# A hand-written engine order for the second layer of a fused attention and two-layer network kernel

## The chip, the cores and the metric

The kernel runs on one core of a Trainium2 chip. The metric is the device time of one execution in microseconds. Before the change it is 1295.35 us, the median of three runs (1294.71 to 1295.54).

## The reference

Chunked attention (chunks of 64, softmax inside each chunk) feeds two dense layers; the second one ends in a softmax-weighted normalization. Tokens: 4608. All data are float32. The part that the change touches is the second layer:

```python
x = _attn_ref(q, k, v)                      # 4608 x 512
h = x @ w_in;  y = (h * np.cos(h)) @ w_out  # first layer, 512 -> 2048 -> 512
h = y @ w_in2                               # second layer, 512 -> 1024
e = np.exp(h - np.max(h, axis=-1, keepdims=True))
solu = h * e / (np.sum(e, axis=-1, keepdims=True) + 1e-09)
mu = np.mean(solu, axis=-1, keepdims=True)
var = np.mean((solu - mu) ** 2, axis=-1, keepdims=True)
out = (((solu - mu) / np.sqrt(var + 1e-06)) * g_ln) @ w_out2
```

## The kernel before, in words

TensorE multiplies in a reduced float format, so every operand is split into a high part (ACT copies it into the format) and a low part (DVE subtracts): `split`, L115. A product is then three matmuls: high by high, high by low, low by high.

The first layer works on blocks of 512 tokens. `evac_y` (L690) writes its result y to DRAM as seven operands per pair of token tiles, the operands of a Strassen-like scheme with seven products in place of eight.

The second layer works on 18 **pairs** of tiles of 128 tokens. A pair has four **segments** (`pair`, L890). Each computes one or two of the seven products (`prod`, L874: 6 matmuls each; segment 2 has one product, the others two) into a PSUM tile of two banks and adds them into the two halves of two tiles h2 on DVE. Segment 0 also copies its first product into h2 on ACT (L918). Some of the sums yield a running maximum as well, called tp. PSUM tiles come from `ps_y` (two buffers) and `ps_a` (one) in turn, so a segment of pair 3 or later takes the buffer of the segment three before it. `load_y` (L726) and `split_y` (L731) fetch and split a pair's y.

For each tile e of a pair, `stats` (L935) negates the maximum (nm, DVE), takes the exp (ACT, L941), multiplies (DVE, L945), squares (ACT, L950) and takes the variance to the power -0.5 on POOL (L955, L956). `norm` (L959) applies it (ACT), `blocks32` (L970) transposes blocks of 32 on DVE into bt. After every second pair `shuffle` (L985) moves bt by 16 DMAs on SP's queue into four tiles lt of 128 tokens. `split_ln` (L996) splits such a tile into lh (ACT) and ll (DVE). `mm_o` (L1001) multiplies it by the output weights in two halves of 12 matmuls, and `store` (L1012) copies the result (ACT) and sends it out by four DMAs.

What sets the order: at L1106 one loop runs over the segments of all pairs from pair 3, segment 1. `segment(i, seg)` (L1020) does segment seg of pair i, the stats of one tile of pair i-1 at even segments and its norm and blocks at odd ones, and loads or splits the next y. Beside it run the two halves of output tile t = 2i - LAG2 + seg // 2, with LAG2 = 7. The first three pairs and segment 0 of pair 3 are done inside the loop of the first layer. In all of this the instructions' places on each engine are left to a scheduler, which takes a ready instruction by priority. `InOrder` (L99) is a wrapper of an engine whose instructions stay in the order in which they are written while `ordered[0]` is true; before the change it is true only for the first stage of the kernel.

Of the kernel before, what the change touches and what calls it, by code (L numbers as in the profile page):

```python
# [29 lines left out]
def kernel(  # L30
# [695 lines left out]
    def load_y(i):  # L726
        t = sp_.tile([P, 7 * 256], F32, tag="st", name="yr")
        nc.sync.dma_start(out=t, in_=y_dram[i // 2][i % 2])
        yr[i] = t
# [19 lines left out]
    if True:  # L749
# [124 lines left out]
        def prod(i, ps, operand, key):  # L874
            for kk in range(2):
                a, b = (y[i][operand][:, kk * P:(kk + 1) * P] for y in (yh, yl))
                whi, wlo = w2in[key, kk]
                nc.tensor.matmul(out=ps, lhsT=a, rhs=whi, start=kk == 0, stop=False)  # L878
                nc.tensor.matmul(out=ps, lhsT=a, rhs=wlo, start=False, stop=False)  # L879
                nc.tensor.matmul(out=ps, lhsT=b, rhs=whi, start=False, stop=kk == 1)  # L880
# [9 lines left out]
        def pair(i, seg):  # L890
# [4 lines left out]
            if seg == 0:  # L895
                h2tile(i, 0)
                h2tile(i, 1)
# [3 lines left out]
            def add(o, ps, other, top=None):  # L901
                if top is None:
                    nc.vector.tensor_tensor(out=o, in0=ps, in1=other, op=ALU.add)
                else:
                    m, before = top
                    nc.vector.tensor_tensor_reduce(  # L906
# [8 lines left out]
            if seg == 0:  # L915
                prod(i, x, 0, "w11")
                prod(i, y, 1, "w12")
                nc.scalar.activation(out=b0, in_=x, func=AF.Copy)  # L918
                add(a0, y, b0, peak(0, 0))
            elif seg == 1:  # L920
                prod(i, x, 4, "s2")
                prod(i, y, 5, "s3")
                add(b0, x, b0)
                add(a1, y, b0)
            elif seg == 2:
                prod(i, x, 3, "s1")
                add(b1, x, a1, peak(1, 0))
                add(b0, x, b0)
            else:
                prod(i, x, 6, "w22")  # L930
                prod(i, y, 2, "s4")
# [3 lines left out]
        def stats(i, e):  # L935
            h2 = hA.pop((i, e))
            nm = ap_.tile([P, 1], F32, tag="nm", name="nm", bufs=4)
            ss = ap_.tile([P, 1], F32, tag="ss", name="ss", bufs=4)
            nc.vector.tensor_scalar(out=nm, in0=tops.pop((i, e, 1)), scalar1=-1.0, scalar2=None, op0=ALU.mult)
            ex = ap_.tile([P, 1024], F32, tag="t", name="e", bufs=2)  # L940
            nc.scalar.activation(out=ex, in_=h2, func=AF.Exp, bias=nm, accum_out=ss)  # L941
            nc.vector.tensor_scalar(out=ss, in0=ss, scalar1=1e-9, scalar2=None, op0=ALU.add)
            nc.vector.reciprocal(out=ss, in_=ss)
            mu = ap_.tile([P, 1], F32, tag="mu", name="mu", bufs=4)
            nc.vector.scalar_tensor_tensor(  # L945
                out=h2, in0=h2, scalar=ss, in1=ex, op0=ALU.mult, op1=ALU.mult, accum_out=mu
            )
            nc.vector.tensor_scalar(out=mu, in0=mu, scalar1=-1.0 / F2, scalar2=None, op0=ALU.mult)
            va = ap_.tile([P, 1], F32, tag="va", name="va", bufs=4)
            nc.scalar.activation(out=ex, in_=h2, func=AF.Square, bias=mu, accum_out=va)  # L950
            nc.vector.tensor_scalar(
                out=va, in0=va, scalar1=1.0 / F2, scalar2=1e-6, op0=ALU.mult, op1=ALU.add
            )
            rs = ap_.tile([P, 1], F32, tag="rs", name="rs", bufs=4)
            nc.gpsimd.tensor_tensor(out=rs, in0=va, in1=nhalf, op=ALU.pow)  # L955
            nc.gpsimd.tensor_tensor(out=mu, in0=mu, in1=rs, op=ALU.mult)  # L956
            solu[i, e], nmu[i, e], rstd[i, e] = h2, mu, rs

        def norm(i, e):  # L959
            so = solu[i, e]  # L960
            nc.scalar.activation(
                out=so, in_=so, func=AF.Identity, scale=rstd.pop((i, e)), bias=nmu.pop((i, e))
            )

# [3 lines left out]
        def blocks32(i, e):  # L970
# [8 lines left out]
            if j:  # L979
                nc.vector.transpose(out=blks[j][4][:, :, n], in_=src)  # L980
            else:
                for c in range(4):
                    nc.vector.transpose(out=blks[j][c][:, :, n], in_=src[:, 8 * c:8 * (c + 1)])
# [12 lines left out]
        def split_ln(j, a):  # L996
            hi, lo = wtile(F32R, "lh"), wtile(F32R, "ll")
            split(lnp.pop((j, a)), hi[:], lo[:])
            lnh[j, a], lnl[j, a] = (x.rearrange("p (f c) -> p f c", c=P) for x in (hi, lo))

        def mm_o(j, a, half):  # L1001
# [3 lines left out]
            for f in range(half * NF2 // 2, (half + 1) * NF2 // 2):  # L1005
                hi, lo = lnh[j, a][:, f], lnl[j, a][:, f]
                whi, wlo = w2out[f]
                nc.tensor.matmul(out=o, lhsT=hi, rhs=whi, start=(f == 0), stop=False)  # L1008
                nc.tensor.matmul(out=o, lhsT=hi, rhs=wlo, start=False, stop=False)  # L1009
                nc.tensor.matmul(out=o, lhsT=lo, rhs=whi, start=False, stop=(f == NF2 - 1))  # L1010

        def store(j, a):  # L1012
            s = gp.tile([P, DM], F32, tag="gh", name="os")
            nc.scalar.activation(out=s, in_=ops.pop((j, a)), func=AF.Copy)
# [28 lines left out]
        for n in range(NSTEP + LAG + 1):  # L1043
# [53 lines left out]
            if rest >= 6:  # L1097
# [6 lines left out]
        first_seg = 4 * EARLY + 1  # L1104
        split_ln(0, 0)
        for x in range(first_seg, 2 * (NI + LAG2) + 4):  # L1106
            i, seg = divmod(x, 4)
            segment(i, seg)
            t, half = 2 * i - LAG2 + seg // 2, seg % 2
            if half == 0:  # L1110
                if 0 <= t + 1 < NI:
                    split_ln(*divmod(t + 1, SUB))
                if 0 <= t - 1 < NI:
                    store(*divmod(t - 1, SUB))
            if 0 <= t < NI:
                mm_o(*divmod(t, SUB), half)
# [27 lines left out]
```

## Time and profile before

| | |
|---|---|
| median of three runs | 1295.35 us (1294.71 to 1295.54) |
| the profiled execution, its own time | 1296.76 us |
| its span, first to last instruction | 1295.0 us |
| mean granted clock of TensorE | 0.987 |
| PE busy | 1251.0 us, 97% |
| DVE busy | 953.8 us, 74% |
| ACT busy | 834.3 us, 64% |
| second-layer matmuls of `mm_o` | 864, of them in the profile 288 at each of L1008, L1009, L1010 |

The second layer overlaps the first layer's end up to about 929 us and then has the chip to itself. A row of the timeline has the start in us from the span's start, the duration, the engine, the line, the operation with output and inputs, and in brackets the engine's idle time before it and what released it. A line L105 is that of the wrapper `InOrder`, so tiles tell such instructions apart. A matmul's 0.39 us is its own duration; matmuls overlap, and their starts are closer together.

### The profile page before, as it was taken

The page shows a single profiled execution, that of the slowest core. Times are in us where ns is not written, and L with a number is a line of the kernel's source. Part 1 is how long each engine was busy: PE and PEld are TensorE (multiplying, and loading weights), DVE is VectorE, ACT ScalarE, POOL GpSimd, SP SyncE. Part 2 cuts the span into 40 slices and gives each one's busy share as a digit, 9 for nine tenths or more (in the row PEclk, how much of TensorE's full clock was granted, in tenths as well). Part 3 has the DMA queues.
Part 4 walks back from the last instruction along what each step waited for, and adds up shares of the span by engine and source line. Part 5 has one row for each costly group of instructions (what it writes and reads, how often), then busy time and mean ns, then how long its engine had stood idle before and what let it go on. Part 6 is the DMA issues. An engine that isn't in the chain of part 4 may idle for free.

```text
span 1295.0 us, 20476 instructions
## 1 busy us (share of the span) xinstructions
PE 1251.0 (97%) x7556; PEld 1007.4 (78%) x7556; DVE 953.8 (74%) x1532; ACT 834.3 (64%) x1231; POOL 124.4 (10%) x271
## 2 busy tenths in 40 slices
PE   5899999999999999999999999999979999999998
PEld 4666778888887777878788888888868888888886
DVE  5987989776778879858868866657786677766851
ACT  5877886656666757647757656557666565666552
POOL 0000000022022022022022012000010000000000
PEclk7999999999999999999999999999989999999999
DMA  9952354342352553562562610641564453435224
GB/s 241 218 112 97 98 141 97 82 102 37 71 155 79 136 148 85 143 146 61 118 129 73 142 31 17 211 159 67 165 179 104 132 147 100 128 90 148 62 70 104
DMA packets 247075, 149.75 MB, mean 116 GB/s; under 512 B 179904, under 2 KB 220352, under 8 KB 245440
## 3 DMA queue, kind: packets, MB, share of 16 engines
q1 hardware_dynamic: 240736, 142.02, 42.8%
q0 software_dynamic: 6144, 6.30, 2.0%
q8 instruction: 59, 0.97, 0.3%
q14 instruction: 40, 0.33, 0.1%
q10 hardware_dynamic: 96, 0.13, 0.0%
HBM read 83.63 MB, written 39.58 MB: 95 GB/s over the span
## 4 chain that ended last, share of the span: by engine, by line
PE 67%; DVE 17%; ACT 8%; issue 3%; DMA 3%; SPq 2%; POOL 0%; DVEq 0%; ACTq 0%; POOLq 0%
PE h L615 6%; PE h L616 6%; PE h L617 6%; PE y L678 6%; PE y L677 6%; PE y L679 6%; PE o L1010 5%; PE o L1008 5%; PE o L1009 5%; PE h L878 4%; PE h L880 4%; PE h L879 4%; DVE z L105 3%; DVE r L630 2%; SPq L105 2%
## 5 line engine op out<-in xcount | busy, mean ns | idle before, releaser
L615 PE MATMUL h<-xh,whi 128*128 128x512 f32 x576 | 228.6, 397 | 2.4 <-ACT xh L105 1.4
L617 PE MATMUL h<-xh,wlo 128*128 128x512 f32 x576 | 225.7, 392 | 0.0
L616 PE MATMUL h<-xl,whi 128*128 128x512 f32 x576 | 225.2, 391 | 0.0
L678 PE MATMUL y<-gl,whi 128*128 128x512 f32 x544 | 214.2, 394 | 4.3 <-DVE gl L105 4.1
L677 PE MATMUL y<-gh,whi 128*128 128x512 f32 x544 | 214.1, 397 | 1.7 <-ACT gh L105 1.1
L679 PE MATMUL y<-gh,wlo 128*128 128x512 f32 x544 | 212.5, 391 | 0.0
L639 ACT ACTIVATE r<-r 128x512 f32<-128x512 f32 x144 | 91.0, 632 | 117.9 <-DVE r L633 117.6
L534 POOL DMA_DIRECT2D ptb<-ptr x192 | 95.4, 504 | 698.4 <-DVE ptr L527 344.1
L105 ACT ACTIVATE gh<-hs 128x512 fp32r<-128x512 f32 x136 | 85.6, 629 | 102.7 <-DVE hs L647 97.2
L647 DVE SCALAR_TENSOR_TENSOR hs<-r,hs 128x512 f32<-128x512 f32 x136 | 93.1, 684 | 65.1 <-ACT r L640 64.8
L630 DVE SCALAR_TENSOR_TENSOR r<-kt,hs 128x512 f32<-128x512 int32 x144 | 99.1, 688 | 47.7 <-ACT kt L629 47.4
L615 PEld LDWEIGHTS h<-xh,whi 128*128 128x128 f32 x576 | 108.6, 189 | 27.6 <-issue 2.3
L616 PEld LDWEIGHTS h<-xl,whi 128*128 128x128 f32 x576 | 108.7, 189 | 23.9 <-issue 1.4
L105 DVE TENSOR_TENSOR gl<-hs,gh 128x512 fp32r<-128x512 f32 x136 | 93.1, 685 | 46.2 <-ACT gh L105 46.0
L617 PEld LDWEIGHTS h<-xh,wlo 128*128 128x128 f32 x576 | 108.6, 188 | 23.1 <-DVE wlo L105 0.2
L678 PEld LDWEIGHTS y<-gl,whi 128*128 128x128 f32 x544 | 102.4, 188 | 29.9 <-DVE gl L105 9.5
L677 PEld LDWEIGHTS y<-gh,whi 128*128 128x128 f32 x544 | 102.2, 188 | 26.1 <-ACT gh L105 2.8
L679 PEld LDWEIGHTS y<-gh,wlo 128*128 128x128 f32 x544 | 102.4, 188 | 21.2 <-DVE wlo L105 0.3
L1008 PE MATMUL o<-whi,lh 128*128 128x512 f32 x288 | 113.4, 394 | 1.6 <-ACT lh L105 1.6
L1010 PE MATMUL o<-whi,ll 128*128 128x512 f32 x288 | 113.3, 393 | 0.8 <-DVE ll L105 0.8
L1009 PE MATMUL o<-wlo,lh 128*128 128x512 f32 x288 | 113.0, 392 | 0.0
L878 PE MATMUL h<-whi,yh 128*128 128x512 f32 x252 | 99.6, 395 | 10.5 <-DVE tp L906 10.5
(113 smaller groups left out, 2162.2 us busy)
## 6 DMA issues: line engine op xcount, KB each, us to landing
lt<-bt SPq DMA_DIRECT2D x144, 128.0 KB
yr<-yd SPq DMA_DIRECT2D x18, 896.0 KB
yd<-ts SPq DMA_DIRECT2D x18, 512.0 KB
out<-os SPq DMA_DIRECT2D x142, 64.0 KB
vi<-in_v SPq DMA_DIRECT2D x64, 128.0 KB
qi<-in_q SPq DMA_DIRECT2D x224, 32.0 KB
ki<-in_k SPq DMA_DIRECT2D x224, 32.0 KB
ptb<-ptr POOLq DMA_DIRECT2D x192, 32.0 KB, 1.7
```

The lines of the kernel that those rows point to most:

```text
L105: ins = getattr(self.engine, name)(*args, **kwargs)
L615: nc.tensor.matmul(out=t, lhsT=wa, rhs=xh[j][:, kk, :], start=(kk == 0), stop=False)
L616: nc.tensor.matmul(out=t, lhsT=wa, rhs=xl[j][:, kk, :], start=False, stop=False)
L617: nc.tensor.matmul(out=t, lhsT=wb, rhs=xh[j][:, kk, :], start=False, stop=(kk == KD - 1))
L630: nc.vector.scalar_tensor_tensor(out=r, in0=kt, scalar=-TWO_PI_HI, in1=h, op0=ALU.mult, op1=ALU.add)
L677: nc.tensor.matmul(out=o, lhsT=wa, rhs=a, start=head, stop=False)
L678: nc.tensor.matmul(out=o, lhsT=wa, rhs=b, start=False, stop=False)
L679: nc.tensor.matmul(out=o, lhsT=wb, rhs=a, start=False, stop=last)
L878: nc.tensor.matmul(out=ps, lhsT=a, rhs=whi, start=kk == 0, stop=False)
L1008: nc.tensor.matmul(out=o, lhsT=hi, rhs=whi, start=(f == 0), stop=False)
L1009: nc.tensor.matmul(out=o, lhsT=hi, rhs=wlo, start=False, stop=False)
L1010: nc.tensor.matmul(out=o, lhsT=lo, rhs=whi, start=False, stop=(f == NF2 - 1))
```

## The change

The scheduler no longer sets the order of the second layer from pair 3 on. `ordered[0]` is set, all matmuls, ACT and DVE instructions of the second layer go through the wrappers, and a new loop writes the order out, one step per pair i. Segment 0 of pair 3 moves from the first layer's loop into it. `pair` is cut into `pair_mm`, `pair_copy` and `pair_sum`, and `stats` into `st_exp`, `st_mul`, `st_square` and `st_var`, with the same instructions in each. `split_ln` can do its high (half 0) or low part (half 1) alone. The load of pair 4's y goes to POOL's queue, ahead of the loop; later loads stand at the end of a step.

```diff
-            if rest >= 6:
+            if 6 <= rest < 6 + 4 * EARLY:
                 segment((rest - 6) // 4, (rest - 6) % 4)
...
         LAG2 = 7
-        first_seg = 4 * EARLY + 1
-        split_ln(0, 0)
-        for x in range(first_seg, 2 * (NI + LAG2) + 4):
-            i, seg = divmod(x, 4)
-            segment(i, seg)
-            t, half = 2 * i - LAG2 + seg // 2, seg % 2
-            if half == 0:
-                if 0 <= t + 1 < NI:
-                    split_ln(*divmod(t + 1, SUB))
-                if 0 <= t - 1 < NI:
-                    store(*divmod(t - 1, SUB))
-            if 0 <= t < NI:
-                mm_o(*divmod(t, SUB), half)
+        load_y(EARLY + 1, nc.gpsimd)
+        ordered[0] = True
+        for i in range(EARLY, NI // 2 + (LAG2 + 1) // 2 + 1):
+            p, t = i - 1, 2 * i - LAG2
+            new, old = i < NPAIR, EARLY - 1 <= p < NPAIR
...
+            if i == EARLY:
+                split_o(t + 1, 0)
+            if new:
+                pair_mm(i, 0)
+            half_o(t, 0)
+            if old:
+                st_exp(p, 0)
+                st_exp(p, 1)
+            store_o(t - 1)
+            split_o(t + 1, 1)
+            if old:
+                st_mul(p, 0)
+                st_square(p, 0)
+            if new:
+                pair_copy(i)
+            if old:
+                st_mul(p, 1)
+            if new:
+                pair_sum(i, 0)
+            if old:
+                st_square(p, 1)
+                st_var(p, 0)
+                st_var(p, 1)
+            if new:
+                pair_mm(i, 1)
+            half_o(t, 1)
+            if old:
+                norm(p, 0)
+                norm(p, 1)
+                blocks32(p, 0)
+            if new:
+                pair_sum(i, 1)
+            if i == EARLY:
+                split_y(i + 1)
+            if old:
+                blocks32(p, 1)
+                if p % 2:
+                    shuffle(p // 2)
+            split_o(t + 2)
+            if new:
+                pair_mm(i, 2)
+            half_o(t + 1, 0)
+            if EARLY < i and i + 1 < NPAIR:
+                split_y(i + 1)
+            if new:
+                pair_sum(i, 2)
+            store_o(t)
+            split_o(t + 3, 0)
+            if new:
+                pair_mm(i, 3)
+            half_o(t + 1, 1)
+            if new:
+                pair_sum(i, 3)
+            if i + 2 < NPAIR:
+                load_y(i + 2)
```

`split_o`, `half_o` and `store_o` call `split_ln`, `mm_o` and `store` where their tile t exists.

PE where the first output tile (o) meets the last segment of pair 3 (h2_9255; in the changed kernel h2_9266). Before:

```order
L879 MATMUL h2_9212<-wlo_8369,yh_9143 128x512
L880 MATMUL h2_9212<-whi_8368,yl_9144 128x512
L878 MATMUL h2_9255<-whi_8472,yh_9143 128x512
L1008 MATMUL o_9242<-whi_8852,lh_9188 128x512
L1009 MATMUL o_9242<-wlo_8853,lh_9188 128x512
L879 MATMUL h2_9255<-wlo_8473,yh_9143 128x512
```

And now:

```order
L105 MATMUL o_9247<-whi_8856,lh_9156 128x512
L105 MATMUL o_9247<-wlo_8857,lh_9156 128x512
L105 MATMUL o_9247<-whi_8856,ll_9157 128x512
L105 MATMUL h2_9266<-whi_8472,yh_9143 128x512
L105 MATMUL h2_9266<-wlo_8473,yh_9143 128x512
```

The last segment stood right behind segment 2; it now stands behind twelve matmuls of output tile 0, and no output matmul stands inside it.

DVE at the same place: the end of pair 2's stats and pair 3's first sum, whose product is h2_9149 (in the changed kernel h2_9159). Before:

```order
L945 SCALAR_TENSOR_TENSOR h2_8929,mu_9229<-h2_8929,ss_9223,e_9225 128x1024
L951 TENSOR_SCALAR va_9177<-va_9177 128x1
L948 TENSOR_SCALAR mu_9229<-mu_9229 128x1
L951 TENSOR_SCALAR va_9232<-va_9232 128x1
L980 STREAM_TRANSPOSE bt_9208<-h2_8928 128x32x32
L980 STREAM_TRANSPOSE bt_9208<-h2_8929 128x32x32
L906 ISA h2_9150,tp_9165<-h2_9149,h2_9151 128x512
```

And now:

```order
L105 SCALAR_TENSOR_TENSOR h2_8941,mu_9193<-h2_8941,ss_9178,e_9180 128x1024
L105 TENSOR_SCALAR mu_9193<-mu_9193 128x1
L105 ISA h2_9190,tp_9198<-h2_9159,h2_9191 128x512
L105 ISA tp_9198 128x1
L105 TENSOR_SCALAR va_9188<-va_9188 128x1
L105 TENSOR_SCALAR va_9200<-va_9200 128x1
L105 STREAM_TRANSPOSE bt_9225<-h2_8940 128x32x32
```

The sum moves ahead of both transposes and of the variances.

DVE at the last sums of pair 17, the last pair (their product is h2_11836; in the changed kernel h2_11841). Before:

```order
L906 ISA h2_11701,tp_11849<-h2_11836,h2_11701,tp_11716 128x512
L906 ISA tp_11849 128x1
L980 STREAM_TRANSPOSE bt_11773<-h2_11507 128x32x32
L906 ISA h2_11702,tp_11851<-h2_11836,h2_11702,tp_11794 128x512
L906 ISA tp_11851 128x1
L980 STREAM_TRANSPOSE bt_11773<-h2_11508 128x32x32
L939 TENSOR_SCALAR nm_11867<-tp_11849 128x1
```

And now:

```order
L105 ISA h2_11753,tp_11866<-h2_11841,h2_11753,tp_11761 128x512
L105 ISA tp_11866 128x1
L105 ISA h2_11754,tp_11868<-h2_11841,h2_11754,tp_11829 128x512
L105 ISA tp_11868 128x1
L105 TENSOR_SCALAR nm_11883<-tp_11866 128x1
```

The two transposes of pair 16 no longer stand between pair 17's last sums and nm.

## Rows read from the trace of the kernel before

**Rows 1.** Busy time by stage: us; PE, PEld, DVE, ACT, POOL; clock, DMA share, GB/s

```profile
1000.00:1050.00 50.00, 49.45 (x218) 40.61 (x218) 36.70 (x80) 29.60 (x42) 3.71 (x10) 1.00 0.50 141
```

**Rows 2.** Timeline of PE, the end: start us, us, line, operation

```profile
1245.38 0.39 PE L1008 MATMUL o<-whi,lh 128*128 128x512 f32 x1
...
1264.19 0.39 PE L1010 MATMUL o<-whi,ll 128*128 128x512 f32 x1
...
1290.30 0.39 PE L1010 MATMUL o<-whi,ll 128*128 128x512 f32 x1
```

**Rows 3.** Timeline of PE, the handover

```profile
938.26 0.39 PE L880 MATMUL h<-whi,yl 128*128 128x512 f32 x1
...
945.25 0.79 PE L878 MATMUL h<-whi,yh 128*128 128x512 f32 x1 [6.60 <-DVE tp L906]
...
950.22 0.39 PE L1010 MATMUL o<-whi,ll 128*128 128x512 f32 x1
```

**Rows 4.** Busy time in three short stretches of the handover, columns as in rows 1

```profile
936.00:938.00 2.00, 2.00 (x10) 1.69 (x9) 1.85 (x7) 1.10 (x2) 0.00 (x0) 1.00 1.03 284
...
946.00:948.00 2.00, 2.00 (x7) 1.49 (x5) 1.84 (x4) 0.00 (x0) 0.00 (x0) 0.50 0.80 305
...
952.00:954.00 2.00, 2.00 (x11) 1.64 (x10) 0.80 (x2) 0.00 (x0) 0.00 (x0) 1.00 0.00 0
```

**Rows 5.** The chain that ended last, one piece: first and last of seven

```profile
988.32 0.60 ACT h L918
...
1238.38 0.60 ACT h L918
```

**Rows 6.** Timeline of PE in one pair

```profile
989.70 0.50 PE L878 MATMUL h<-whi,yh 128*128 128x512 f32 x1 [0.55 <-DVE tp L906]
```

**Rows 7.** Timeline of PE after the last shuffle

```profile
1267.47 0.72 PE L1010 MATMUL o<-whi,ll 128*128 128x512 f32 x1 [0.53 <-DVE ll L105]
...
1270.97 0.40 PE L1009 MATMUL o<-wlo,lh 128*128 128x512 f32 x1
```

**Rows 8.** Timeline of DVE and ACT, the last pair and the last shuffle

```profile
1246.30 1.24 DVE L980 STREAM_TRANSPOSE bt<-h 128x1024 f32<-128x1024 f32 x1
...
1256.80 2.48 DVE L980 STREAM_TRANSPOSE bt<-h 128x1024 f32<-128x1024 f32 x2 [0.98 <-ACT h L961]
...
1265.11 1.05 ACT L105 ACTIVATE lh<-lt 128x1024 fp32r<-128x1024 f32 x1
...
1266.19 1.23 DVE L105 TENSOR_TENSOR ll<-lt,lh 128x1024 fp32r<-128x1024 f32 x1 [6.92 <-ACT lh L105]
```

**Rows 9.** Timeline of ACT, the handover

```profile
934.73 1.16 ACT L941 ACTIVATE e<-h,nm 128x1024 f32<-128x1024 f32 x1 [4.60 <-DVE nm L939]
...
938.05 1.15 ACT L950 ACTIVATE e<-h,mu 128x1024 f32<-128x1024 f32 x1 [0.94 <-DVE ss L943]
...
940.87 2.45 ACT L961 ACTIVATE h<-h,mu,rs 128x1024 f32<-128x1024 f32 x2
...
943.23 0.58 ACT L918 ACTIVATE h<-h 128x512 f32<-128x512 f32 x1
```

**Rows 10.** Timeline of DVE, the handover

```profile
938.14 1.28 DVE L945 SCALAR_TENSOR_TENSOR h<-h,ss,e 128x1024 f32<-128x1024 f32 x1
...
942.12 2.48 DVE L980 STREAM_TRANSPOSE bt<-h 128x1024 f32<-128x1024 f32 x2 [0.98 <-ACT h L961]
...
944.52 0.65 DVE L906 CUSTOM_DVE_ANT_0 h<-h,h 128x512 f32<-128x512 f32 x1
```

**Rows 11.** Timeline of SP's queue, the handover

```profile
935.70 8.76 SPq L990 DMA_DIRECT2D lt<-bt  x11
...
944.50 1.07 SPq L728 DMA_DIRECT2D yr<-yd  x2
```

**Rows 12.** Tile ptb: issues by POOL (duration ns min/median/max), and landing

```profile
L534 POOL DMA_DIRECT2D ptb<-ptr x192: 498/498/838, 268.5 to 794.6; - x192
...
DMA to landing us min/median/max: 1.6/1.7/8.5
```

More of the change, by code (lines that the diff above doesn't have):

```diff
@@ L724, with load_y @@
     yr, yh, yl = {}, {}, {}
[L726 removed]
+    def load_y(i, queue=None):
         t = sp_.tile([P, 7 * 256], F32, tag="st", name="yr")
[L728 removed]
+        (queue or nc.sync).dma_start(out=t, in_=y_dram[i // 2][i % 2])
         yr[i] = t
@@ L877, in prod @@
                 whi, wlo = w2in[key, kk]
-                nc.tensor.matmul(out=ps, lhsT=a, rhs=whi, start=kk == 0, stop=False)
-                nc.tensor.matmul(out=ps, lhsT=a, rhs=wlo, start=False, stop=False)
-                nc.tensor.matmul(out=ps, lhsT=b, rhs=whi, start=False, stop=kk == 1)
+                pe.matmul(out=ps, lhsT=a, rhs=whi, start=kk == 0, stop=False)
+                pe.matmul(out=ps, lhsT=a, rhs=wlo, start=False, stop=False)
+                pe.matmul(out=ps, lhsT=b, rhs=whi, start=False, stop=kk == 1)
         def h2tile(i, e):
@@ L888, in h2tile, with pair_mm @@
             return hA[i, e]
-        def pair(i, seg):
+        h2ps = {}
+        def pair_mm(i, seg):
             c = 4 * i + seg
@@ L895, in pair, with pair_copy, pair_sum @@
             if seg == 0:
-                h2tile(i, 0)
-                h2tile(i, 1)
+                prod(i, x, 0, "w11")
+                prod(i, y, 1, "w12")
+            elif seg == 1:
+                prod(i, x, 4, "s2")
+                prod(i, y, 5, "s3")
+            elif seg == 2:
+                prod(i, x, 3, "s1")
+            else:
+                prod(i, x, 6, "w22")
+                prod(i, y, 2, "s4")
+            h2ps[i, seg] = x, y
+        def pair_copy(i):
+            h2tile(i, 0)
+            h2tile(i, 1)
+            act.activation(out=hA[i, 1][:, HALVES[0]], in_=h2ps[i, 0][0], func=AF.Copy)
+        def pair_sum(i, seg):
+            x, y = h2ps.pop((i, seg))
             a, b = hA[i, 0], hA[i, 1]
@@ new lines, in pair, with col, st_exp @@
+        def pair(i, seg):
+            pair_mm(i, seg)
+            if seg == 0:
+                pair_copy(i)
+            pair_sum(i, seg)
+        small_ = {}
+        def col(i, e, name):
+            t = small_[i, e, name] = ap_.tile([P, 1], F32, tag=name, name=name, bufs=4)
+            return t
+        def st_exp(i, e):
+            nm, ss = col(i, e, "nm"), col(i, e, "ss")
+            dve.tensor_scalar(out=nm, in0=tops.pop((i, e, 1)), scalar1=-1.0, scalar2=None, op0=ALU.mult)
+            ex = small_[i, e, "ex"] = ap_.tile([P, 1024], F32, tag="t", name="e", bufs=2)
+            act.activation(out=ex, in_=hA[i, e], func=AF.Exp, bias=nm, accum_out=ss)
@@ L994, in shuffle, with split_ln @@
                 lnp[j, a] = l
[L996 to L999, printed above, removed]
+        def split_ln(j, a, half=None):
+            if half != 1:
+                lnh[j, a], lnl[j, a] = wtile(F32R, "lh"), wtile(F32R, "ll")
+            split(lnp[j, a], lnh[j, a][:], lnl[j, a][:], half=half)
         def mm_o(j, a, half):
```

77 lines of the change are left out of this document (40 added, 37 removed).

## The prediction

> **What bounds the kernel now.** I read the busy time by stage first. In the second layer TensorE (PE) is busy 49.45 us of 50 at full granted clock, VectorE (DVE) 36.70 and ScalarE (ACT) 29.60 [rows 1]. So PE sets the end there, and only what interrupts it can be won. A busy share does not tell PE's pace, so the timeline comes next. Between its last second-layer product and the stall near the end PE issues 84 matmuls from 1245.38 to 1264.19 us, 83 steps of 0.2266 us [rows 2]. I take 0.2266 us for a matmul throughout.
>
> The changed stretch begins at the handover. After the matmul at 938.26 PE has 1464 matmuls to go: 12 products of pair 3, 42 for each of 14 pairs, 24 for each of 36 output tiles. At the pace above they take 331.7 us. From 938.49 (one step after that matmul) to 1290.53 (one step after the last, [rows 2]) 352.0 us pass. So 20.3 us are lost, and I can place nearly all of them.
>
> - Handover: the next matmul starts at 945.25 where 938.49 was due, 6.76 us late, and waits for DVE's tp, the first sum of pair 3 [rows 3]. After that pause the granted clock is 0.50, which is 1.2 GHz [rows 4]: 10 matmuls take 4.97 us to 950.22 instead of 2.27 [rows 3]. That is 2.70 more, 9.5 us in all. Some 0.35 us follow where the y operands of pair 4 come late.
> - Every second pair: ACT's copy of the first product recurs from 988.32 to 1238.38 in six periods of 41.68 us [rows 5]; 180 matmuls need 40.79. The 0.89 us between them is PE waiting for the tp of the same segment, because the last segment's product is put in front of the output matmuls that could cover the wait [rows 6]. There are seven such places: 6.2 us.
> - The last shuffle: the matmul due at 1264.42 and the next run late, the third only at 1267.47, 2.60 us lost; eight steps to 1270.97 then take 3.50 us instead of 1.81 [rows 7]. Together 4.3 us.
>
> The sum is 9.5 + 0.35 + 6.2 + 4.3 = 20.3 us.
>
> **The change part by part.** No matmul, sum or transfer is added or removed; all of it is order and queue. So I follow each wait in the new order.
>
> *Steady pairs.* I set time 0 at a pair's first matmul. PE now has a fixed row: product 0, 12 output matmuls, product 1, 12, product 2 (6 matmuls), 12, product 3, 12; products start at 0, 5.44, 10.88 and 14.95 us and the next pair at 20.39. A product needs the PSUM tile of the product three earlier, so product 3 needs the first sum of its own pair. That sum comes behind two exps, a store, a square and the copy on ACT. Worked from the durations in [rows 8 to 10]: the previous pair's last sums end at -1.1, the exps at 1.6, the copy at 4.1, the first sum at 4.9. Product 3 starts at 14.95, so the old wait has 10 us of cover. The y split of the next pair ends near 14.5, needed at 20.39. DVE fits 27% idle time into its row [rows 1], so it does not fall behind. I take the seven 0.89 us at nothing: gain 6.2 us. If that cover failed, the 6.2 us would remain (a rival below).
>
> *Handover.* DVE now does the first split of an output operand between nm and the exps. ACT stood idle 4.60 us there, and the first exp ended at 935.9 [rows 9], so a split of 1.23 us [rows 8] starting at 934.76 ends when DVE would have gone on anyway. Costed at nothing; if the exps came sooner it would cost 1.2 us. Then the order that matters: in the old one DVE did two transposes (2.48 us) from 942.12 before the sum of pair 3 at 944.52 [rows 10]; ACT did both squares and both norms before the copy at 943.23 [rows 9]. In the new one the copy follows the first square (938.05 + 1.15, so 939.3 to 939.9) and the sum follows the second product with e, which ends at 939.4: about 940.0 to 940.75. Meanwhile PE no longer waits with product 3 next in line: 12 output matmuls of tile 0 come first, 938.49 to 941.2. Product 3 starts at 941.2, the second 12 at 943.9, pair 4 at 946.65. The 6.76 and the 2.70 us go.
>
> *What is late next there* is pair 4's y. Its load of 0.92 MB stood on SP's queue, which issued it at 944.50, behind 11 shuffle transfers that took from 935.70 [rows 11]. It moves to POOL's queue, past SP's 16 shuffle and 2 last yd transfers. On POOL it stands ahead of the two small operations of pair 2's variance, which now wait behind its issue. Its buffer comes free when the first yd writes have landed and DVE's last ts sum is done, about 935.5. The trace has no such load from POOL; the nearest rows are the 192 small ones, 504 ns to issue, 1.7 us to land, 8.5 at most [rows 12]. I scale the issue to four of those, 2 us, to 937.6; the variance operations are due at 940.9, so 3 us are spare. For landing there are two bounds: alone at the 284 GB/s that the stretch moves [rows 4], 3.2 us, at 940.8; behind everything on SP's queue, at about 951, since DMA is quiet from 952 on [rows 4]. I take an equal share with SP's queue, 6.5 us, landing at 944.1, nearest to the small loads, which did not wait for SP's queue to empty. ACT reaches yh at 944.2 anyway (behind both norms); yh's first part takes 1.05 and yl's 1.23 [rows 8], so yl is ready at 946.8. PE needs it at its third matmul, 947.1. Then pair 4's first 12 output matmuls need the split of tile 1, which DVE ends at about 950.2 behind yl and a transpose; PE is there at 949.8: 0.4 us. Handover gain: 9.5 + 0.35 - 0.4 = 9.4 us.
>
> A load from POOL could also be held back by DVE, busy without a pause until 940.9; that is part of the late-load rival below. The Trainium skill (SBUF — State Buffer, section "SBUF: two separate sides") has a rule of this kind: GpSimd writes the descriptors of its own loads, and can't while DVE runs an operation in a mode that takes the port which the two share. The rows lean against it: DVE needs 1.28 us for 1024 columns there [rows 10], no less than elsewhere, so no such mode shows.
>
> *Tail.* The old order put both transposes of pair 16 between the last sums of pair 17 and its nm (one at 1246.30 [rows 8]; they delay the chain by 2.33 us). The new order has done them earlier. From pair 17's last product (its last matmul, one step before the first of [rows 2], ends at 1245.54) to the split of tile 32 (ends 1267.42, [rows 8]) the chain took 21.9 us; without 2.33 it takes 19.55. The cover is 84 matmuls, 19.03 us, plus two matmuls of tile 32 that do not need the low part. I leave 0.5 us, since ACT now holds that split ahead of a store. Such a short wait leaves the clock alone: a stretch with a 0.55 us wait in it [rows 6] is at 1.00 [rows 1]. Gain 4.3 - 0.5 = 3.8 us.
>
> *Sum.* 6.2 + 9.4 + 3.8 = 19.4 us off the profiled execution's 1296.76 us gives 1277.4. That execution is 1.4 us above the median of the runs, 1295.35; against the median the forecast is **1276.0 us**.
>
> **The rivals.**
> 1. *Late load.* Pair 4's y lands between 947.5 (POOL first issues at DVE's pause near 941) and 951 (behind SP's queue). For: DMA is saturated there, 1.03 busy [rows 4]. Against: the small loads' 1.7 us. yl comes 2.8 to 6.5 us after PE wants it, and 1.7 to 2.7 us of slow matmuls follow as at both long pauses: 4.5 to 9 us, so 1280.5 to 1285.
> 2. *The pair's wait stays*, moved to another product, at its old 0.89 us: 1282.2. Against: 10 us of cover.
> 3. *The tail keeps its stall*, if the transfers, not the DVE chain, set it: ACT took the split at 1265.11, right after a store. Then 3.8 us come back: 1279.8.
> 4. *Slower.* In the fixed row ACT takes the split of the next shuffled tile ahead of the next pair's exps. If the shuffle lands late, exps, sums and the y split all move. At the end of the program the first split came 5.8 us after the transposes' end at 1259.28 [rows 8]. In the steady row the transposes end at 11.15, so it starts at 16.9 and leaves 1.7 us before the exps and 5.9 us before PE needs y. From 13.4 us of landing on PE pays each microsecond, seven times. At 16.2 us (2.8 too many, seven times: 19.6) the gain is gone; at 17.2, 1303. Only SP standing still on buffers or stores would do it.
> 5. *Nothing moves*: would need the built order to be the old one; the order shown above excludes it.
>
> **How the numbers follow.** Forecast with small residues 0.70 (1274.5 to 1279), late load 0.14, pair wait 0.05, tail 0.04, slower 0.05, near no change by several of these together 0.02. The range 1274.5 to 1285 takes in the first four. Its low end is the sum with neither residue (1275.1) and a little for the spread between runs. 0.2%, 2.6 us, is what the measurement can tell. Faster 0.93, same 0.02, slower 0.05.
>
> **What would show it.** Right: PE's pause before the last product of pair 3 gone, no stretch at 1.2 GHz there, ACT's copy at equal distances near 20.4 us in every pair, PE waiting under 1 us for tile 32, last matmul near 1271. Wrong: PE waiting for yh or yl of pair 4 (rival 1), for tp in the pairs (2), for lh of tile 32 (3), or ACT's exps starting right behind a late lh (4).

## The result, and the profile after

| | before | after |
|---|---|---|
| median of the runs | 1295.44 us (1294.71 to 1295.91, 4 runs) | 1279.47 us (1278.09 to 1280.71, 4 runs) |
| profiled execution | 1296.76 us | 1278.09 us |
| matmul after pair 3's third product, last matmul | 938.49 (due), 1290.30 us | 936.60, 1271.56 us |
| lost against 0.2266 us a matmul | 20.3 us | 3.4 us |

The ratio is 0.9877, 95% interval [0.986, 0.9894]: 16.0 us by the medians. The forecast was 1276.0 us in a range of 1274.5 to 1285.

The last line of the table is the measure that I use for every run below: from the first output matmul of tile 0 to the start of the last matmul there are 1463 steps, 331.5 us at the pace of [rows 2]; what passes beyond that is lost. It leaves out what lies before the change, which differs between executions: in the profiles of the runs below the first output matmul starts between 936.60 and 939.92 us (e6, where its place is another, aside). In after's profile that earlier part was 1.9 us shorter than in before's, so of the 18.7 us between the two profiled executions 16.9 are the change.

The pairs first. The changed kernel's busy time in the stretch of [rows 1] (us; PE, PEld, DVE, ACT, POOL; clock, DMA share, GB/s):

```profile
1000.00:1050.00 50.00, 50.00 (x223) 41.40 (x221) 37.09 (x77) 29.70 (x43) 2.86 (x8) 1.00 0.56 141
```

and its chain of work that ended last, where [rows 5] had ACT's copy once in 41.68 us (start us, us, what):

```profile
1101.61 2.72 PE o L105 x12
1104.33 2.72 PE h L105 x12
1107.05 2.72 PE o L105 x12
...
1120.65 1.36 PE h L105 x6
```

PE is busy 50.00 of 50 us, and no other engine stands in the chain. The 0.89 us waits are gone.

Then the two ends. The timeline of PE in the changed kernel, to be held against [rows 3] and [rows 7] (start us, us, engine, line, operation, idle time before it and what ended it):

```profile
936.60 0.39 PE L105 MATMUL o<-whi,lh 128*128 128x512 f32 x1
...
939.32 0.39 PE L105 MATMUL h<-whi,yh 128*128 128x512 f32 x1
...
945.39 0.50 PE L105 MATMUL h<-whi,yl 128*128 128x512 f32 x1
...
948.17 0.50 PE L105 MATMUL o<-whi,lh 128*128 128x512 f32 x1 [0.18 <-ACT lh L105]
...
949.43 0.50 PE L105 MATMUL o<-whi,ll 128*128 128x512 f32 x1 [0.53 <-DVE ll L105]
...
1253.54 0.39 PE L105 MATMUL o<-whi,ll 128*128 128x512 f32 x1
1255.32 0.50 PE L105 MATMUL o<-whi,lh 128*128 128x512 f32 x1 [1.39 <-ACT os L105]
```

The last product of pair 3 starts at 939.32, right where twelve matmuls put it; the pause of 6.76 us is gone, and the slow stretch with it. What is left there is three short waits, 1.6 us in all: 0.3 for yl, the low part of pair 4's y (945.39), and 1.3 for output tile 1 (948.17, 949.43). At the end the two waits for tile 32 are gone, but a new one stands at 1255.32, before tile 33: 1.7 us, and it waits for ACT's copy of tile 31, not for an operand.

Who is late, by the timelines of ACT, DVE, SP's queue and POOL in the changed kernel:

```profile
943.02 1.80 ACT L105 ACTIVATE yh<-yr 128x1024 fp32r<-128x1024 f32 x2 [1.00 <-DMA yr<-yd]
947.06 1.06 ACT L105 ACTIVATE lh<-lt 128x1024 fp32r<-128x1024 f32 x1 [2.24 <-DMA lt<-bt]
...
1254.67 0.60 ACT L105 ACTIVATE os<-o 128x512 f32<-128x512 f32 x1 [5.56 <-DMA out<-os]
```
```profile
937.92 0.69 DVE L105 CUSTOM_DVE_ANT_0 h<-h,h 128x512 f32<-128x512 f32 x1
...
948.15 1.23 DVE L105 TENSOR_TENSOR ll<-lt,lh 128x1024 fp32r<-128x1024 f32 x1 [0.79 <-ACT lh L105]
```
```profile
933.81 11.26 SPq L1020 DMA_DIRECT2D lt<-bt  x11
...
1241.13 10.05 SPq L1020 DMA_DIRECT2D lt<-bt  x16
1251.27 22.17 SPq L1048 DMA_DIRECT2D out<-os  x26
```
```profile
933.98 0.59 POOL L728 DMA_DIRECT2D yr<-yd  x1 [18.86 <-DMA lt<-bt]
```

DVE's first sum ends at 938.6, 0.7 us ahead of the product that needs its buffer. Tile 1's split is late because ACT waits 2.24 us for its shuffle transfers; the eleven transfers take 11.26 us on SP's queue instead of 8.76 [rows 11], while pair 4's y comes over POOL's queue. DVE then waits 0.79 us for ACT's high part of tile 1. At the end ACT's copy of tile 31 waits 5.56 us for a store buffer: there are two, and the writes of tile 29 stand on SP's queue behind the sixteen transfers of the last shuffle.

### The profile page after: what moved, and what is told of

Its sections match the earlier page's. It is cut to its first block, busy times and chain, and to the rows that moved or that the text cites. A ratio compares the mean times of both kernels' runs of the same rounds, so it can differ in the third digit from the quotient of the medians.

```text
span 1276.3 us, 20453 instructions
## 1 busy us (share of the span) xinstructions
PE 1243.5 (97%) x7556; PEld 1004.8 (79%) x7556; DVE 961.1 (75%) x1532; ACT 832.7 (65%) x1231; POOL 123.2 (10%) x272
## 4 chain that ended last, share of the span: by engine, by line
PE 66%; DVE 17%; ACT 8%; SPq 3%; DMA 3%; issue 3%; POOL 0%; DVEq 0%; ACTq 0%; POOLq 0%
PE o L105 13%; PE h L105 12%; PE h L615 6%; PE h L617 6%; PE h L616 6%; PE y L677 6%; PE y L678 6%; PE y L679 6%; DVE z L105 3%; DVE r L630 2%; SPq L105 2%; DVE hs L647 2%; DVE r L633 2%; DVE gl L105 1%; PE x L105 1%
## 5 line engine op out<-in xcount | busy, mean ns | idle before, releaser
L622 ACT ACTIVATE hs<-h 128x512 f32<-128x512 f32 x144 | 84.4, 586 | 31.5 <-PE h L617 20.9
```

What stands on the lines that cost most here:

```text
L622: nc.scalar.activation(out=h, in_=hps.pop(n), func=AF.Copy)
```

## The experiments

All start from the changed kernel. Each ratio is against the kernel before, run beside it; "lost" is the measure above.

| run | median us | ratio [95%] | first output matmul, last matmul | lost us |
|---|---|---|---|---|
| changed kernel | 1279.47 | 0.9877 [0.986, 0.9894] | 936.60, 1271.56 | 3.4 |
| e1 y on SP | 1284.85 | 0.9914 [0.9899, 0.9929] | 938.61, 1279.21 | 9.1 |
| e2 tail store | 1278.10 | 0.9859 [0.9844, 0.9874] | 938.72, 1272.04 | 1.8 |
| e3 y between | 1280.27 | 0.9877 [0.9862, 0.9891] | 937.09, 1272.73 | 4.1 |
| e4 e2 and e3 | 1280.44 | 0.988 [0.9863, 0.9896] | 938.15, 1272.76 | 3.1 |
| e5 old ACT, DVE at handover | 1284.76 | 0.9911 [0.9896, 0.9926] | 939.15, 1279.10 | 8.4 |
| e6 old PE at handover | 1280.51 | 0.9888 [0.9871, 0.9904] | 942.03, 1272.60 | 4.0 |
| e7 old PE in the pairs | 1277.89 | 0.9859 [0.9844, 0.9873] | 938.75, 1271.98 | 1.7 |
| e8 ACT, DVE free | 1349.69 | 1.0411 [1.0395, 1.0426] | 939.92, 1342.56 | 71.1 |
| e9 late sum | 1280.66 | 0.9877 [0.9862, 0.9892] | 937.65, 1273.89 | 4.7 |
| e10 late sum, old PE | 1284.67 | 0.9907 [0.9889, 0.9925] | 939.04, 1279.23 | 8.7 |
| e11 shuffle on POOL | 1284.77 | 0.9908 [0.9888, 0.9929] | 939.45, 1277.35 | 6.4 |
| e12 copy behind a store | 1295.76 | 0.9996 [0.9986, 1.0006] | 936.91, 1288.87 | 20.4 |

In e6 the last product goes ahead of the first output matmul: 1451 steps, and its wait of 2.2 us is added.

### e1: pair 4's y on SP's queue again

```
-        load_y(EARLY + 1, nc.gpsimd)
+        load_y(EARLY + 1)
```

> Undoes one part of the change: the load of pair 4's y goes back from POOL's queue to SP's, behind the eleven shuffle transfers; nothing else differs from the changed kernel (median 1279.5 us, ratio 0.9877). Theory A, the place of this load is worth several microseconds: without the second queue the eleven transfers take about 8.8 us again instead of 11.26, the load is issued near 942.6 and lands 4 to 6 us later, yl is ready near 949 to 951 where TensorE wants it at 945.2; a pause of 4 to 6 us, up to 2.7 us of 1.2 GHz behind it, less the 1.6 us that TensorE now waits there for tile 1. Net 4 to 7 us more: 1283.5 to 1286.5, ratio 0.991 to 0.993. Rival B, the same bytes go through the same DMA engines whatever the queue: y lands by 945 and the time stays within 1 us, ratio 0.987 to 0.989.

Its timelines of SP's queue and of PE, and PE's granted clock (last but two) in a stretch behind the pause:

```profile
935.84 8.76 SPq L1020 DMA_DIRECT2D lt<-bt  x11
944.64 8.53 SPq L728 DMA_DIRECT2D yr<-yd  x3
```
```profile
950.74 0.80 PE L105 MATMUL h<-whi,yh 128*128 128x512 f32 x1 [3.81 <-ACT yh L105]
```
```profile
950.50:954.50 4.00, 3.72 (x8) 2.52 (x9) 3.78 (x4) 2.82 (x4) 0.00 (x0) 0.50 0.28 77
```

5.7 us more are lost: a pause of 4.2 us less one step, and some 3 us behind it (matmuls at 1.2 GHz, with short waits for yl among them), less the tile 1 waits that it hides. Theory A holds: without the second queue the handover gives back over half of its gain. The eleven transfers take 8.76 us again, so it was y on the other queue that slowed them. The Trainium skill (DMA: Bandwidth & Descriptors, section "SWDGE vs HWDGE vs iDMA") says that the engines take turns between the queues that POOL's software and the hardware path feed; 11.26 against 8.76 us agrees with such sharing.

### e2: tile 29's writes ahead of the last shuffle

```
                 blocks32(p, 1)
+                if not new:
+                    store_o(t)
                 if p % 2:
                     shuffle(p // 2)
...
-            store_o(t)
+            if new or not old:
+                store_o(t)
```

> One change to the changed kernel: behind pair 17 ACT's copy of output tile 29 and its four writes come ahead of the last shuffle's sixteen transfers on SP's queue, no longer behind them. Theory A, the pause of 1.55 us before tile 33 is a wait for the copy of tile 31, which waits for the buffer of tile 29, whose writes stand behind the shuffle: the pause goes, TensorE runs without a gap to the end, 1.6 us less, near 1277.9, ratio 0.9865. Rival B, the tail is set by the transfers of the last shuffle: TensorE then waits for the operand of tile 32 or 33 instead, the same 1.5 us, ratio 0.9877.

Its busy time at the end, where the changed kernel has PE busy 13.61 of 15 us:

```profile
1245.00:1260.00 15.00, 15.00 (x67) 12.20 (x66) 4.54 (x4) 5.70 (x7) 0.00 (x0) 1.00 0.80 185
```

PE runs to the end without a gap, 1.6 us less are lost. Theory A holds; the shuffle's own transfers were in time.

### e3 and e4: y between the shuffle transfers

```
...
                 lnp[j, a] = l
+                if (j, a) == (0, 1):
+                    load_y(EARLY + 1)
...
-        load_y(EARLY + 1, nc.gpsimd)
```

(the lines left out keep this load and the transfers of tiles 2 and 3 in the written order)

> One change to the changed kernel: pair 4's y is loaded on SP's queue after the shuffle transfers of tiles 0 and 1 and ahead of those of tiles 2 and 3, not on POOL's. Theory A, the 1.64 us that TensorE loses at the handover come from tile 1's shuffle transfers, slowed by the load on the other queue: tile 1 lands near 938, y near 942, yl is done near 945.5 and tile 1's low part near 948, so at most 0.4 us stay: 1.2 to 1.6 us less, near 1278.1, ratio 0.9867. Rival B, the order on DVE (yl and a transpose ahead of tile 1's low part) sets it and not the transfers: 1.0 us or more stay, ratio 0.9875. Rival C, the load on SP comes later than on POOL: yl is late by 1 us or more and the time rises.

Its timelines of SP's queue, ACT and PE:

```profile
937.82 0.53 SPq L728 DMA_DIRECT2D yr<-yd  x1
```
```profile
945.17 1.79 ACT L105 ACTIVATE yh<-yr 128x1024 fp32r<-128x1024 f32 x2 [2.70 <-DMA yr<-yd]
```
```profile
946.28 0.50 PE L105 MATMUL h<-whi,yh 128*128 128x512 f32 x1 [0.87 <-ACT yh L105]
```

Rival C holds in the trace: counted from the first output matmul, the load is issued 3.4 us later than on POOL's queue; it lands at 945.1, and PE now waits for y more than for tile 1. By the lost time that is 0.7 us worse than the changed kernel; the medians, 0.8 apart, overlap. With e2's edit beside it:

> The two edits of the runs with tile 29's writes ahead of the last shuffle and pair 4's y between the shuffle transfers, together. Theory A, the two residues are independent: 2.8 to 3.2 us less than the changed kernel, near 1276.4, ratio 0.9855, and TensorE at most 0.5 us late from pair 3's third segment to the end. Rival B, one of them only moves its wait to the other: 1.6 us or less.

3.1 us are lost: the tail's gain stays, the handover is 1.3 us worse than in e2. Theory A's time does not come, but not for rival B's reason: neither edit moves its wait to the other place, e3's is simply no gain.

### e5 and e6: which order took the handover's wait

e5 puts ACT's and DVE's old order back in the step of pair 3:

```
-            if new:
+            if new and i > EARLY:
                 pair_copy(i)
...
-            if new:
+            if new and i > EARLY:
                 pair_sum(i, 0)
...
+            if i == EARLY:
+                blocks32(p, 1)
+                pair_copy(i)
+                pair_sum(i, 0)
             if new:
                 pair_sum(i, 1)
...
```

> Undoes the order of ACT and DVE at the handover alone: in the step of pair 3, both squares and both norms come ahead of the copy and both transposes ahead of the first sum, as before the change; TensorE keeps the new order with twelve output matmuls ahead of the last product. Theory A, both orders are needed: the first sum ends near 944.1, the last product is due at 939.3, so TensorE pauses 4.8 us and up to 2.7 us of 1.2 GHz follow, less the 1.6 us that it waits now for tile 1: 4 to 6 us more, 1283.5 to 1285.5, ratio 0.991 to 0.9925. Rival B, TensorE's order alone took the old wait away: no difference, ratio 0.9877. Rival C, ACT's and DVE's order alone did: 9 us more, 1288.5.

e6 puts PE's old order back there (`pair_mm(i, 3)` ahead of `half_o(t + 1, 0)`):

> Undoes TensorE's order at the handover alone: in the step of pair 3 the last product stands right behind the third one, ahead of all output matmuls, as before the change; ACT and DVE keep the new order. Theory A: the product is due at 936.6 and the first sum ends at 938.6, a pause of 2.0 us, with up to 2.7 us of 1.2 GHz behind it, less the 1.6 us of waiting for tile 1 that this hides: 0.4 to 3.1 us more, 1280 to 1282.5, ratio 0.988 to 0.990. Rival B, TensorE's order carried the whole handover gain: 9 us more, 1288.5.

PE behind the pause of e5, then of e6, with the busy time and clock of the microseconds after it:

```profile
946.09 0.79 PE L105 MATMUL h<-whi,yh 128*128 128x512 f32 x1 [4.06 <-DVE tp L105]
```
```profile
946.00:949.00 3.00, 2.91 (x7) 2.33 (x8) 2.86 (x6) 1.20 (x2) 0.00 (x0) 0.50 1.06 236
```
```profile
939.16 0.50 PE L105 MATMUL h<-whi,yh 128*128 128x512 f32 x1 [1.92 <-DVE tp L105]
```
```profile
939.00:942.00 3.00, 2.84 (x12) 2.36 (x13) 0.92 (x5) 2.63 (x4) 1.44 (x4) 1.00 1.01 306
```

Both forecasts A hold. Undone alone, ACT's and DVE's order costs 5.0 us of lost time, PE's 0.6 (in e6 by the trace only: its medians overlap those of the changed kernel). In e6 the pause is 2.1 us, the clock stays at 2.4 GHz, and the waits for yl and tile 1 vanish behind it, so most of the price comes back.

### e7, e9, e10, e12: what made the pairs wait

e7, from pair 4 on:

```
                 pair_mm(i, 2)
+            if EARLY < i < NPAIR:
+                pair_mm(i, 3)
             half_o(t + 1, 0)
...
-            if new:
+            if new and not (EARLY < i < NPAIR):
                 pair_mm(i, 3)
```

> Undoes TensorE's order in the pairs 4 to 17: the last product of every pair stands ahead of the twelve output matmuls of the other half, as it did in every second pair before; ACT and DVE keep the new order, and the handover keeps all of the new order. Theory A, the sum comes early by the order of ACT and DVE (5 us into a pair, the product now at 12.2): no wait, within 0.5 us, ratio 0.9877. Rival B, TensorE's order carried the 6.2 us of the pairs: 1285.6, ratio 0.9925.

No pair waits, so PE's order alone did not carry the 6.2 us. The tail's pause is gone too, which nothing foretold: the last product of pair 17 stands 2.7 us (twelve matmuls) earlier in PE's row, so the last shuffle is issued 2.4 us earlier, counted from the first output matmul (302.1 against 304.5 us), and with it the writes behind it.

e9 moves ACT's copy behind both norms and DVE's first sum behind both transposes, in the pairs 4 to 17 (their old places are taken out):

```
...
+            if EARLY < i < NPAIR:
+                blocks32(p, 1)
+                pair_copy(i)
+                pair_sum(i, 0)
             if new:
                 pair_sum(i, 1)
...
```

> In the pairs 4 to 17 ACT's copy of the first product goes back behind both squares and both norms, and DVE's first sum behind both transposes, the order that the handover had before; TensorE keeps its fixed row, and the step of pair 3 keeps all of the new order. The first sum then comes about 13 us into a pair instead of 4.9. Theory A, TensorE's row covers it: it wants the sum at 14.95 us, so no wait, and the time stays within 0.5 us of the changed kernel (1279.5, ratio 0.9877; in the trace, the loss behind pair 3's third segment stays at 3.3 us). Rival B, the early sum carries the 6.2 us of the pairs: 1285.7, ratio 0.9925.

e10 is e9 and e7 together:

> Both undone in the pairs 4 to 17: ACT's and DVE's order as in the run with the late sum, and TensorE's last product ahead of the twelve output matmuls as in the run with the old place of the last product. The sum comes about 13 us into a pair, the product is due at 12.2. Theory A, here the pairs' wait is back, 0.5 to 1.3 us in each of 14 pairs: 7 to 18 us more than the changed kernel, 1286.5 to 1297.5, ratio 0.9925 to 1.001, with waits of that size for tp and no long stretch at 1.2 GHz. Rival B, the old wait came from the scheduler's interleaving in every second pair and not from a late sum with an early product: within 1 us, ratio 0.9877.

The only wait for a sum in either run, on PE, first e9, then e10:

```profile
963.57 0.50 PE L105 MATMUL h<-whi,yh 128*128 128x512 f32 x1 [1.19 <-DVE tp L105]
```
```profile
965.22 0.79 PE L105 MATMUL h<-whi,yh 128*128 128x512 f32 x1 [3.91 <-DVE tp L105]
```

That is pair 4, next to the handover, whose stats come late: in e10 ACT's exps start 7.3 us after pair 4's first matmul (954.54, 947.20), in a later pair 2.6 us before it (1116.40, 1118.98). This one pause makes up e9's 1.3 us, and with 1.2 GHz behind it in e10 it puts that run's time between its two theories. The pairs 5 to 17 do not wait, even with both orders undone: theory A of e10 falls. My estimate of 13 us for the late sum was wrong; in e10 it starts 7.4 us into the pair (1126.35, the pair's first matmul at 1118.98). So a sum behind norms and transposes is not what made the kernel before wait. Its timeline of ACT shows what else stood there (the first copy is that of an output tile, the second the pair's):

```profile
1112.88 0.60 ACT L1014 ACTIVATE os<-o 128x512 f32<-128x512 f32 x1 [2.83 <-PE o L1010]
1113.37 0.59 ACT L918 ACTIVATE h<-h 128x512 f32<-128x512 f32 x1
```

The pair's copy stood behind a store that waits for PE's output tile, which ends just ahead of the third product. e12 rebuilds that, with e7's place of the last product (the old places of copy and sum are taken out):

```
...
+            if EARLY < i < NPAIR:
+                store_o(t)
+                pair_copy(i)
+                pair_sum(i, 0)
             if new:
                 pair_sum(i, 1)
...
-            store_o(t)
+            if not EARLY < i < NPAIR:
+                store_o(t)
...
```

> In the pairs 4 to 17 ACT's copy of the first product stands behind the store of the output tile that TensorE ends right before the third product, as it does in every second pair of the old kernel (the store of 1112.88 us, which waits for TensorE, and the copy behind it at 1113.37); TensorE's last product stands right behind the third one, also as there. The rest is the changed kernel. Theory A, this place of the copy is the cause of the old pair wait: the tile's end, store 0.5 us, copy 0.6, sum 0.7 and their starts take 2.2 us, the third product covers 1.36, so 0.8 to 0.9 us of wait for tp in each of 14 pairs, 11 to 13 us, less the 1.7 us of the tail that an early last product saves: 1288 to 1291.5, ratio 0.994 to 0.9965. Rival B, the place of the store is of no matter and only a late sum behind norms and transposes was: as in the run with both orders undone, no wait in the settled pairs, at most 1284.7, ratio 0.991 or below.

PE's waits for tp from 955 to 1250 us in e12 (us in total, times, longest; the kernel before has 3.9, 7 and 0.6 there, e7 none), and one pair in the chain of e12 that ended last:

```profile
PE h L105 <- DVE tp L105: 10.9, 14, 3.7
```
```profile
1173.58 2.73 PE o L105 x12
...
1176.34 0.60 ACT os L105
1176.94 0.50 ACT h L105
...
1177.46 0.69 DVE h L105
...
1178.21 3.02 PE h L105 x12
```

Thirteen pairs have the old wait, each with the very "0.55 <-DVE tp" of [rows 6], 0.82 us lost in each; pair 4 waits 3.73 us and runs slow behind it, and 0.7 us of the tail's pause stay; the expectation had counted neither, and so the time is 4 us above it. The cause is shown: PE's tile ends, ACT stores it, then copies, DVE sums, and PE needs the sum after six matmuls of cover. e7 has the early product without that copy and does not wait. The copy without the early product was not run; the twelve matmuls then ahead of the product, 2.7 us, would cover the 0.82 (an estimate).

### e8: only PE's order by hand

From pair 4 on ACT's and DVE's wrappers let the scheduler place their instructions (`loose` is true in the step of pair 3 alone):

```
-    pe, act, dve = InOrder(nc.tensor), InOrder(nc.scalar), InOrder(nc.vector)
+    pe, act, dve = InOrder(nc.tensor), InOrder(nc.scalar, loose), InOrder(nc.vector, loose)
...
+            loose[0] = i == EARLY
             if new:
                 pair_mm(i, 0)
...
```

> From pair 4 on the places of ACT's and DVE's instructions are left to the scheduler again; TensorE keeps its fixed row, and the step of pair 3 keeps all of the new order. Theory A, either order alone is enough in the pairs: in the old kernel the sum came about 13 us into the pair, and the fixed row wants it only at 14.95; so no wait in the pairs, and at the end the old 1 to 4 us of the last shuffle: 1279.5 to 1283.5, ratio 0.988 to 0.991. Rival B, the order of ACT and DVE carried the 6.2 us: 1285.7 or more, ratio 0.9925 or above.

Its PE, ACT and SP's queue in one pair:

```profile
1031.86 0.79 PE L105 MATMUL o<-whi,lh 128*128 128x512 f32 x1 [6.36 <-ACT lh L105]
```
```profile
1028.41 2.45 ACT L105 ACTIVATE h<-h,mu,rs 128x1024 f32<-128x1024 f32 x2
1030.77 1.99 ACT L105 ACTIVATE lh<-lt 128x1024 fp32r<-128x1024 f32 x2
```
```profile
1011.82 10.23 SPq L1020 DMA_DIRECT2D lt<-bt  x16
```

It is neither theory: the pairs don't wait for a sum, but PE waits 6 to 9 us for lh in every second pair, seven times, with a slow stretch behind each. The transfers were issued by 1022, yet the scheduler put the split behind exps, squares and norms, and PE, in order, can't go past it. An eighth wait, shorter, stands before tile 31: ACT's split is there behind a store that itself waits for PE's tile. So whether PE's row alone would take the old wait away cannot be told beside such pauses; what was measured is that this row for PE alone is worse than no order by hand, 1349.69 against 1296.63 us.

### e11: half of the first shuffle on POOL's queue

```
         load_y(EARLY + 1, nc.gpsimd)
+        shuffle(0, (2, 3), nc.gpsimd)
```

(the shuffle of block 0 itself then issues tiles 0 and 1 alone, and the loads on POOL's queue keep the written order)

> One change to the changed kernel: the eight shuffle transfers of tiles 2 and 3 of the first shuffle go to POOL's queue behind the load of pair 4's y; those of tiles 0 and 1 stay on SP's. Theory A, what TensorE loses at the handover, 1.64 us, is tile 1 and y sharing the transfer engines with tiles 2 and 3, which nobody wants before 955: y lands near 940.5 to 942 and tile 1 by 944, yl is ready at 945.2 and tile 1's low part by 947.9, and 1.2 to 1.6 us go: 1278.1, ratio 0.9867. Rival B, POOL's eight more issues at 0.6 us hold its variance operations, due at 938.8, until 939.4 or later, and with them norms, transposes and yl: no gain or up to 1 us more. Rival C, the next y loads move up on SP's queue in the place of the eight transfers and take their share: no change, ratio 0.9877.

Its POOL and PE:

```profile
937.41 3.41 POOL L1022 DMA_DIRECT2D lt<-bt  x7
945.12 0.49 POOL L1022 DMA_DIRECT2D lt<-bt  x1 [4.30 <-DMA yr<-yd]
945.62 0.57 POOL L984 TENSOR_TENSOR rs<-va,nhalf 128x1 f32<-128x1 f32 x1
```
```profile
950.46 0.76 PE L105 MATMUL h<-whi,yh 128*128 128x512 f32 x1 [2.69 <-DVE h L105]
```

It is rival B, dearer than expected: POOL's ninth transfer in a row waits 4.30 us until y, its first, has landed, the variance operations stand behind it until 945.62, and norms, transposes and the sum that PE's next product waits for come late. It costs 2.9 us in the profiled execution and 5.3 by the medians (e11's runs lie between 1282.64 and 1286.12).

## Why the prediction was right, and where it was short

**Pace and bound: right.** PE bounds the second layer, a matmul takes 0.2266 us, and of the 20.3 us lost before 3.4 still are.

**Pairs, 6.2 us: right in size, half right in cause.** The waits are gone. I named one cause, "because the last segment's product is put in front of the output matmuls that could cover the wait", and did not ask what made the old sum late. e7 shows that the early product alone costs nothing, e10 that it costs nothing in the settled pairs even with the sum behind norms and transposes, e12 that the missing half was ACT's copy behind a store that itself waits for PE. Both halves went with the change, so the size came out right without the second; by the estimate under e12 the late product would have covered the wait alone.

**Handover, 9.4 us: the mechanism right, the residue too small.** Of 9.85 us lost there 1.6 stay, so 8.2 came. Undone one at a time, ACT's and DVE's order costs 5.0 us (e5), PE's 0.6 (e6) and the y load on POOL's queue 5.7 (e1). Together that is more than 8.2, so the parts overlap, and since no run undoes two of them, how the 8.2 split is not shown. The y load came about where I put it (943.0, which is 944.9 on the time axis of the kernel before; I had 944.1), in part by luck: issued in 0.59 us instead of 2, it then took 8.4 us to land instead of 6.5, two misses that nearly cancel. (My sum for yl, 944.2 + 1.05 + 1.23, gives 946.5 and not 946.8; nothing hangs on it.) The failed step is "the split of tile 1, which DVE ends at about 950.2 behind yl and a transpose": I took the order on DVE alone and left its transfers where they were, though I had just given y an equal share with SP's queue. They paid for that share: 11.26 us instead of 8.76, and DVE waited 0.79 us for ACT's high part of tile 1. Without these 0.79 the wait for its low part would be near 0.4 us, as forecast (an estimate). Residue 1.6 instead of 0.4. DMA is busy there either way (share 1.02 from 944 to 950), and e3 and e11 only moved the wait to y or to POOL; an order without any wait was not found.

**Tail, 3.8 us: the chain right in the main, the residue mis-sized and misplaced.** Tile 32 is in time; how much of that the 2.33 us of transposes did was not tested apart. The chain of the kernel before that ended last has one more piece there, which I had only as "right after a store":

```profile
1264.62 0.02 ACT os L1014
...
1265.11 1.06 ACT lh L105
...
1266.19 1.24 DVE ll L105
```

ACT's split of tile 32 stood behind the store of tile 31, which waits for PE, as the copy did in the pairs. In the changed kernel ACT gets tile 32's transfers 4.3 us after the shuffle's first issue (1241.13, 1245.42). The same 4.3 us from the old issue at 1260.22 give 1264.5, and the old split began at 1265.11: by this estimate the store cost 0.6 of the 2.6 us and the late shuffle the rest. The residue, "0.5 us, since ACT now holds that split ahead of a store", was 1.7 us, one tile later and by another path: the new loop issues tile 29's writes behind the last shuffle, and ACT waits for their buffer. I had not followed the moved store's own transfers past the sixteen on SP's queue. e2 shows it. It came 2.6 us instead of 3.8.

**Sum.** 6.2 + 8.2 + 2.6 = 17.0 us, against 19.4; the 2.4 us that are missing are the two residues, 1.2 each. The remaining 1 us between 1276.0 and 1279.47 lies within the runs' own spread of 1278.09 to 1280.71.

**Rivals.** Late load did not come, but its price was right: e1 makes it happen and gives 1284.85 us, inside 1280.5 to 1285. The pair's wait went. The tail's transfers did not set it (e2). The slower case needed a shuffle that lands more than 13.4 us after its transposes; ACT took the split 5.3 us after the transposes ended, at 1125.86 in a pair. e8 shows what such a split costs when it comes late for another reason. Of the port that GpSimd shares with DVE (the Trainium skill, SBUF — State Buffer, section "SBUF: two separate sides") nothing showed at the issue: POOL issued the load in 0.59 us at 933.98, while DVE paused at most 0.12 us at a time until 938.6. Whether it cost a part of the 9.0 us of landing no run here tells.

**A faster version.** e2 and e7 each take the tail's residue: 1278.10 and 1277.89 us, ratio 0.9859 for both. Their intervals overlap that of the changed kernel; the 1.6 to 1.7 us are read from one trace of each.

## What to carry to other kernels

When an engine executes in order, look not only for the latest operand but also for an instruction ahead of it that waits for the engine you want to feed: a store's copy in front of a pair's copy cost 0.82 us a pair, though ACT and DVE were idle over a quarter of the time. If you fix the order of one engine by hand, look at all that feed it (e8 lost 71 us with PE's row alone, the kernel before 20), and follow each moved step's own transfers past what is on their queue. Compare executions from the first changed instruction on: a sum of waits showed 1.6 us that medians with a spread of 2.6 us could not.

## What was not expected of the hardware

- TensorE's granted clock stayed at 1.00 behind a pause of 2.1 us (e6) and of 1.6 us (the changed kernel's tail, 1.00 from 1254 to 1256), and was 0.50 behind pauses of 2.9 us (e11, from 951 to 953), 4.0 us (e1) and 4.2 us (e5). Behind these longer ones 1.7 to 3.3 us more were lost, short waits for operands among them.
- The length of a pause does not settle it. The same two waits, 1.63 us for lh and 0.53 us for ll, stand before tile 32 in the kernel before ([rows 7] has the second) and before tile 31 in e8. Behind them the clock was 0.50 in the one and 1.00 in the other; what made the difference stays open. So 1.7 of the 4.3 us that I counted for the old tail belong to one execution and may be absent in another. First the kernel before, then e8:

```profile
1266.21 0.50 PE L1008 MATMUL o<-whi,lh 128*128 128x512 f32 x1 [1.63 <-ACT lh L105]
```
```profile
1268.00:1271.00 3.00, 3.00 (x9) 2.33 (x8) 1.61 (x2) 1.62 (x2) 0.00 (x0) 0.50 0.86 197
```
```profile
1314.65 0.50 PE L105 MATMUL o<-whi,lh 128*128 128x512 f32 x1 [1.63 <-ACT lh L105]
...
1315.91 0.50 PE L105 MATMUL o<-whi,ll 128*128 128x512 f32 x1 [0.53 <-DVE ll L105]
```
```profile
1316.00:1319.00 3.00, 3.00 (x14) 2.46 (x15) 1.32 (x2) 1.27 (x2) 0.00 (x0) 1.00 0.93 212
```

- A load of 0.92 MB took POOL 0.59 us to issue, hardly more than the 498 ns of the small ones [rows 12]. But the ninth transfer in a row held POOL for 4.30 us until the first had landed (e11).
- The same load landed in 9.0 us from POOL's queue beside a busy SP queue (e11: 8.0) and in some 5 us on SP's queue behind the eleven transfers (e1).
